# DeltaNet followed by a GELU MLP on one core: 32 heads in lockstep on 64x64 tiles, the MLP interleaved, the order list-scheduled

## The chip, the cores and the metric

The kernel runs on one core of one Trainium2 chip. The metric is the device time of one execution in microseconds; lower is better. A run more than 1.5% above the fastest of its kernel counts as slow; ratios use the other, fast runs alone, medians are of all runs. One core has five engines that matter here: TensorE (matmuls, PE in the profile, PEld for its weight loads), VectorE (DVE), ScalarE (ACT), GpSimd (POOL) and SyncE (SP, which here only issues DMA transfers).

## The reference

```python
# q, k, v: (4 batches, 8 heads, 768 tokens, 48); beta: (4, 8, 768)
k_n = k / (np.linalg.norm(k, axis=-1, keepdims=True) + 1e-06)
for t in range(S):                       # S = 768 tokens, one after the other
    y[:, :, t] = einsum('bhd,bhde->bhe', q[:, :, t], state)
    v_old = einsum('bhde,bhd->bhe', state, kt)
    state = state + bt * einsum('bhd,bhe->bhde', kt, vt - v_old)
# x: (3072 tokens, 384) from y, heads side by side
h = x @ w_in                             # 384 -> 2048
g = 0.5 * h * (1 + tanh(c * (h + 0.044715 * h**3)))
return g @ w_out                         # 2048 -> 384
```

Both kernels take 64 tokens at a time (a chunk). Inside a chunk the recurrence becomes a triangular 64x64 system, whose inverse is built by repeated squaring: M and N are the powers of the matrix and of its transpose, L is the inverse so far. Five levels of matmul and eviction (reading the product out of PSUM) follow one another. Only then come the few matmuls with the state S, which one chunk hands to the next: R = v - K S, U = T R, and S + KᵀU.

## The kernel before

Two heads are put on the diagonal of one 128x128 matrix (a pair), so half of every product and of every eviction, the two off-diagonal blocks, is zeros. A column is 8 pairs of one chunk; three columns are in flight. The five levels:

```python
for lev in range(1, 6):                              # cut
    for hf in range(NHALF):                          # two halves of 4 pairs
        for jj in range(NSLOT):
            E("pe", f_matmul(b0[:, jj, :], Nsrc[:, jj, :], Msrc[:, jj, :]), ...)   # 128x128x128
            if not last:
                E("pe", f_matmul(b1[:, jj, :], Msrc[:, jj, :], Nsrc[:, jj, :]), ...)
    yield
    ...
        E("act", f_act(Mdst[:, :, :], b0[:, :, :]), ...)     # evictions of 128x512
        ...
            E("pe", f_matmul(b1[:, jj, :], Mdst[:, jj, :], prev[:, jj, :]), ...)
        E("dve", f_tt(cur[:, :, :], b1[:, :, :], prev[:, :, :], ALU.add), ...)     # LT
    yield
```

The norm is a square and a sum, then a square root on ScalarE and an addition and a reciprocal on VectorE:

```python
E("pool", f_tt(sq_col[:, :, :], Kcv, Kcv, ALU.mult), ...)
E("dve", f_reduce(n1[:, :], sq_col[:, :, :], AX.X, ALU.add), ...)
E("act", f_act(n2[:, :], n1[:, :], ACT.Sqrt), ...)
E("dve", f_tscalar(n1[:, :], n2[:, :], 1e-6, ALU.add), ...)
E("dve", f_recip(n2[:, :], n1[:, :]), ...)
```

All columns are done before the MLP starts. Its GELU is a sigmoid form: two passes of ScalarE and three of VectorE for each block of 128x512.

```python
while nxt < len(tasks) or active:                    # DeltaNet: at most three columns
    while nxt < len(tasks) and len(active) < 3: ...
...                                                  # then the MLP, block by block
E("act", f_act(gb["hs"], hbk), ...)
E("dve", f_stt(gb["gq"], gb["hs"], two_ca, gb["hs"], ALU.mult, ALU.mult), ...)
E("dve", f_stt(gb["garg"], gb["gq"], two_c, gb["hs"], ALU.add, ALU.mult), ...)
E("act", f_act(gb["gs"], gb["garg"], ACT.Sigmoid), ...)
E("dve", f_tt(gb["gT"], gb["gs"], gb["hs"], ALU.mult), ...)
```

## Time and profile before

| | us |
|---|---|
| median of the first 3 runs | 963.94 (956.53 to 969.27) |
| loading, TensorE nearly idle | 0 to 74 |
| DeltaNet | 74 to 667 |
| MLP | 667 to 960 |

From the page of the kernel before: busy time of each engine, TensorE's busy tenths and its granted clock in 40 equal slices of the span, and the chain of work that ended last.

```profile
span 960.0 us, 14337 instructions
PE 569.2 (59%) x5459; PEld 415.1 (43%) x5472; DVE 532.3 (55%) x940; ACT 422.6 (44%) x866; POOL 218.7 (23%) x187
PE   0003667675667663767676768676566656556563
PEclk9999968786787687686776766587667879897987
...
PE 38%; DVE 24%; ACT 12%; issue 10%; SPq 6%; POOL 5%; DMA 3%; DVEq 0%; POOLq 0%; ACTq 0%
```

No engine is near full, and the chain of waits jumps between three of them. After the loading, the clock is rarely at nine or ten tenths. (Its records are only full or half; "warm" below means full clock.) The windows view of the kernel before gives busy us and instructions of each engine in the three stages, then the clock and the DMA share:

```profile
core 0: us, PE busy (x) PEld busy (x) DVE busy (x) ACT busy (x) POOL busy (x), PEclk, DMA share, GB/s
0.00:74.00 74.00, 3.88 (x32) 3.45 (x32) 10.39 (x7) 1.70 (x3) 21.53 (x22) 1.00 0.60 94
74.00:667.00 593.00, 392.58 (x4763) 342.76 (x4764) 360.29 (x642) 294.62 (x643) 197.12 (x165) 0.75 0.13 27
667.00:960.00 293.00, 172.76 (x668) 68.86 (x678) 161.65 (x291) 126.24 (x221) 0.00 (x0) 0.81 0.06 20
```

And three of its costliest groups (line, engine, operation, out<-in, shapes, count | busy us, mean ns | idle before it):

```profile
L134 ACT ACTIVATE MA<-mb 128x512 bf16<-128x512 f32 x240 | 134.6, 604 | 148.0 <-PE mb L118 147.0
L130 DVE SCALAR_TENSOR_TENSOR Kres<-Kres 128x512 bf16<-128x512 bf16 x192 | 127.3, 688 | 87.8 <-ACT Kres L134 86.5
L126 DVE TENSOR_TENSOR LT<-mb,LT 128x512 bf16<-128x512 f32 x192 | 123.4, 686 | 77.3 <-PE mb L118 77.3
```

Each of these 128x512 passes costs 0.60 us on ScalarE and 0.69 us on VectorE. The change attacks the number of these passes.

### The profile page before, as it was taken

The page shows a single profiled execution, that of the slowest core. Times are in us where ns is not written, and L with a number is a line of the kernel's source. Part 1 is how long each engine was busy: PE and PEld are TensorE (multiplying, and loading weights), DVE is VectorE, ACT ScalarE, POOL GpSimd, SP SyncE. Part 2 cuts the span into 40 slices and gives each one's busy share as a digit, 9 for nine tenths or more (in the row PEclk, how much of TensorE's full clock was granted, in tenths as well). Part 3 has the DMA queues.
Part 4 walks back from the last instruction along what each step waited for, and adds up shares of the span by engine and source line. Part 5 has one row for each costly group of instructions (what it writes and reads, how often), then busy time and mean ns, then how long its engine had stood idle before and what let it go on. Part 6 is the DMA issues. An engine that isn't in the chain of part 4 may idle for free.

```text
span 960.0 us, 14337 instructions
## 1 busy us (share of the span) xinstructions
PE 569.2 (59%) x5459; PEld 415.1 (43%) x5472; DVE 532.3 (55%) x940; ACT 422.6 (44%) x866; POOL 218.7 (23%) x187
## 2 busy tenths in 40 slices
PE   0003667675667663767676768676566656556563
PEld 0002656564556553656565656664222212222221
DVE  3102757574666574667575757565545547474654
ACT  0002545553546452554545454455434434453443
POOL 3405052523333214415151515030000000000000
PEclk9999968786787687686776766587667879897987
DMA  7554002154000001530000000000001000000000
GB/s 103 97 82 138 11 21 71 33 103 78 1 6 1 5 2 27 82 48 2 1 1 2 1 2 1 2 13 15 15 15 44 1 33 1 33 8 26 14 20 33
DMA packets 119990, 28.57 MB, mean 30 GB/s; under 512 B 114417, under 2 KB 119537, under 8 KB 119537
## 3 DMA queue, kind: packets, MB, share of 16 engines
q1 hardware_dynamic: 107120, 26.44, 13.0%
q10 hardware_dynamic: 12800, 1.21, 1.0%
q8 instruction: 43, 0.70, 0.3%
q14 instruction: 27, 0.21, 0.1%
HBM read 20.55 MB, written 4.72 MB: 26 GB/s over the span
## 4 chain that ended last, share of the span: by engine, by line
PE 38%; DVE 24%; ACT 12%; issue 10%; SPq 6%; POOL 5%; DMA 3%; DVEq 0%; POOLq 0%; ACTq 0%
PE mb L118 37%; SPq L163 6%; DVE LT L126 6%; ACT Kres L134 6%; DVE Kres L130 5%; DVE NB L138 3%; DMA out_dram<-Kres 3%; DVE Kres L126 2%; ACT QT L134 2%; PE mb L122 2%; POOL IMN L126 2%; ACT KnT L134 2%; POOL sq_col L126 2%; DVE MA L126 2%; DVE NB L126 1%
## 5 line engine op out<-in xcount | busy, mean ns | idle before, releaser
L134 ACT ACTIVATE MA<-mb 128x512 bf16<-128x512 f32 x240 | 134.6, 604 | 148.0 <-PE mb L118 147.0
L130 DVE SCALAR_TENSOR_TENSOR Kres<-Kres 128x512 bf16<-128x512 bf16 x192 | 127.3, 688 | 87.8 <-ACT Kres L134 86.5
L126 DVE TENSOR_TENSOR LT<-mb,LT 128x512 bf16<-128x512 f32 x192 | 123.4, 686 | 77.3 <-PE mb L118 77.3
L118 PE MATMUL mb<-W,Kres 128*128 128x384 bf16 x384 | 99.7, 397 | 108.8 <-DVE Kres L126 80.0
L118 PE MATMUL mb<-MA,NB 128*128 128x128 bf16 x960 | 145.5, 254 | 0.0
L118 PE MATMUL mb<-NB,MA 128*128 128x128 bf16 x768 | 125.9, 253 | 8.8 <-DVE LT L126 8.3
L134 ACT ACTIVATE Kres<-mb 128x512 bf16<-128x512 f32 (+1 forms) x120 | 68.2, 574 | 113.2 <-PE mb L118 83.1
L118 PEld LDWEIGHTS mb<-W,Kres 128*128 128x128 bf16 x384 | 36.6, 111 | 173.9 <-DVE Kres L126 127.3
L118 PE MATMUL mb<-LT,MA 128*128 128x128 bf16 x768 | 68.5, 238 | 64.1 <-DVE NB L138 61.5
L118 PEld LDWEIGHTS mb<-MA,NB 128*128 128x128 bf16 x960 | 104.4, 117 | 0.0
L118 PEld LDWEIGHTS mb<-NB,MA 128*128 128x128 bf16 x768 | 87.7, 116 | 20.6 <-DVE LT L126 13.8
L118 PEld LDWEIGHTS mb<-LT,MA 128*128 128x128 bf16 x768 | 52.0, 107 | 74.9 <-ACT NB L134 43.2
L134 ACT ACTIVATE Kres<-Kres 128x512 bf16<-128x512 bf16 x96 | 59.8, 628 | 50.9 <-DVE Kres L130 50.8
L122 PE MATMUL mb<-identb,Qb_col 128*96 128x128 bf16 x192 | 38.9, 292 | 56.9 <-POOL Qb_col L138 56.9
L122 PE MATMUL mb<-identb,Kb_col 128*96 128x128 bf16 x192 | 27.9, 293 | 72.6 <-ACT QT L134 72.6
L138 DVE CAST NB<-mb 128x512 bf16<-128x512 f32 x96 | 65.1, 678 | 3.6 <-PE mb L118 3.6
L126 POOL TENSOR_TENSOR IMN<-ident,NB 128x512 bf16<-128x512 f32 x48 | 55.2, 1156 | 30.7 <-DVE NB L126 30.0
L122 PEld LDWEIGHTS mb<-identb,Qb_col 128*96 128x96 bf16 x192 | 34.2, 181 | 57.5 <-POOL Qb_col L138 57.5
L134 ACT ACTIVATE NB<-mb 128x512 bf16<-128x512 f32 x96 | 58.6, 611 | 0.0
L126 DVE TENSOR_TENSOR Kres<-Kres 128x512 bf16<-128x512 bf16 x96 | 40.0, 422 | 32.3 <-ACT Kres L134 29.6
L122 PEld LDWEIGHTS mb<-identb,Kb_col 128*96 128x96 bf16 x192 | 19.1, 169 | 80.9 <-ACT QT L134 80.9
L118 PE MATMUL mb<-Vres,W 128*128 128x512 bf16 x184 | 53.0, 414 | 0.9 <-issue 0.7
(70 smaller groups left out, 1059.5 us busy)
## 6 DMA issues: line engine op xcount, KB each, us to landing
Qres<-in_q_dram SPq DMA_DIRECT2D x64, 72.0 KB, 2.5
Kres<-in_k_dram SPq DMA_DIRECT2D x64, 72.0 KB, 2.6
out_dram<-Kres SPq DMA_DIRECT2D x24, 192.0 KB, 1.9
Vres<-in_v_dram SPq DMA_DIRECT2D x48, 72.0 KB, 2.6
xsb<-in_moe_w_in_dram SPq DMA_DIRECT2D x3, 1024.0 KB, 4.9
xsb<-in_moe_w_out_dram SPq DMA_DIRECT2D x3, 960.0 KB, 5.2
Vres<-in_v_dram ACTq DMA_DIRECT2D x16, 72.0 KB, 2.9
Bres<-in_beta_dram SPq DMA_DIRECT2D x48, 1.5 KB, 2.4
```

What stands on the lines that cost most here:

```text
L118: return lambda t: t.matmul(out, lhsT, rhs, start=start, stop=stop)
L122: return lambda t: t.transpose(out, in_, idm)
L126: return lambda e: e.tensor_tensor(out, a, b, op)
L130: return lambda e: e.scalar_tensor_tensor(out, in0, scalar, in1, op0, op1)
L134: return lambda s: s.activation(out, in_, func)
L138: return lambda e: e.tensor_copy(out, in_)
L163: return lambda sp: sp.dma_start(out, in_)
```

## The change

The intent has five parts. Heads no longer share a 128x128 matrix: each head's 64x64 product runs on one quarter (tile) of the array, so a 128x512 eviction carries 16 heads' matrices and no zeros. All 32 heads of a chunk go together through 12 chunks. Loads are per chunk, so the work starts after the first chunk's loads. The MLP of finished tokens is interleaved, with one GELU pass on ScalarE. And the order of every engine is fixed in advance by a list scheduler from planned durations; each engine's queue then runs in that order, with waits where a result is needed.

The diff rewrites the whole file; this is its core, with cuts.

```diff
+LAT = {"pe": 0.25, "dve": 0.12, "act": 0.14, "pool": 0.16, "sp": 0.0}
+class Plan:                                          # list scheduler, cut
+    def op(self, cost, fns, reads=(), writes=(), prio=0.0, alloc=(), dma=None, lat=0.0):
+...
+def mm_pe(n_ins, cols):                              # planned duration of small matmuls
+    return {"pe": 0.02 + n_ins * max(0.030, (cols / 2.4 + 32) * 0.5e-3)}
+...
+# the norm: the square root has become a power on GpSimd
+op({"pool": 0.6}, {"pool": f_tt(sr[j], ss[j], half, ALU.pow)}, ...)
+op({"dve": 0.1}, {"dve": lambda e: e.tensor_scalar(ss[j], sr[j], 1e-6, None, op0=ALU.add)}, ...)
+op({"dve": 0.2}, {"dve": lambda e: e.reciprocal(rn[j], ss[j])}, ...)
+# K and Q of 32 heads are transposed by one DMA, issued by SyncE
+op({"sp": 1.1}, {"sp": f_dma(KQT[i]..., KQ[i]..., True)}, ..., lat=4.0)
+...
+def nl(...):                                         # one level: N and L of 8 pairs
+    return [(bank(h1, p // 4)[64*a:64*a+64, ...], M[64*a:64*a+64, p, :],
+             NL[64*a:64*a+64, p, :, :]..., True, True, True)
+            for p in range(8) for a in range(2)]     # a alternates: two tiles of the array
+...
+# GELU in one pass
+op({"act": 0.6}, {"act": f_act(G[:, fc, :], lambda h=h: bank(h), ACT.Gelu_apprx_tanh)}, ...)
-E("dve", f_stt(gb["gq"], gb["hs"], two_ca, gb["hs"], ALU.mult, ALU.mult), ...)
-E("dve", f_stt(gb["garg"], gb["gq"], two_c, gb["hs"], ALU.add, ALU.mult), ...)
-E("act", f_act(gb["gs"], gb["garg"], ACT.Sigmoid), ...)
```

## The prediction

> **What bounds the kernel now.** No engine: the page gives TensorE 59% busy, VectorE 55%, ScalarE 44%. Three phases follow one another (windows view): loading, 0–74 us, with TensorE almost idle; DeltaNet, 74–667 us (TensorE 393 us busy, VectorE 360, ScalarE 295); MLP, 667–960 us (TensorE 173, VectorE 162, ScalarE 126). The chain of waits is 38% TensorE, 24% VectorE, 12% ScalarE: one dependency chain of matmul, eviction, matmul, filled by only three columns in flight. The granted clock is 0.75 in DeltaNet and 0.81 in the MLP: start to start, a 128-column matmul takes 56 ns warm and 107 ns cold, a 48-column one 25 and 40 ns (my reading of start times). The Trainium skill, "TensorE: Matmul & The Clock Gate", Part 1, names these two states; the clock records here are only 1.0 and 0.5, so they agree.
>
> **What the change does.**
> - 64x64 tiles instead of block-diagonal 128x128 pairs: an eviction of 128x512 now carries 8 useful pairs, not 4. PSUM-reading VectorE work falls from 480 large passes to 274 (274 x 0.685 us = 188 us); 34+12 passes of 768 columns (about 0.95 us, estimated from 349 ns at 192 and 685 ns at 512) are 44 us; the rest about 28 us: **VectorE 260 us** (532 before).
> - Gelu becomes one ScalarE pass; two STT (688 ns), a multiply (422 ns) and a copy per tile go. **ScalarE about 150 us** (230 x 0.60 plus small; 423 before).
> - GpSimd: 24 x 1.16, 24 x 1.47, 12 x 0.82, 24 masks of 1024 at about 2 us: **about 125 us**.
> - TensorE: 5,474 matmuls become 7,107. 4,896 of 48 or 64 columns at 27–30 ns, 1,536 of 128 columns at 40–45 ns (estimates from the warm 25 and 56 ns, two tiles overlapping), MLP 288 x 0.216 + 384 x 0.163 = 125 us: **about 340 us warm**, more when cold. TensorE becomes the fullest engine, about 28 us per chunk of 64 tokens with its MLP share.
> - MLP runs inside DeltaNet, so its 293 us stop being a separate phase; only the last tile (16 gelu blocks, 4 output blocks) remains as a tail.
> - Loading shrinks to the first chunk: first matmuls near 28 us instead of 74.
>
> **Sum.** Start 28 us (load, norm, GpSimd scaling, one DMA transpose of 16 blocks, estimated 4–8 us), then 320 us of TensorE work, tail 35 us (DMA transpose, 21 us matmuls, output): 383 us if TensorE never waited warm. It will wait: fixed order from planned costs, eight PSUM banks, six matmul–eviction levels, a clock I expect at 0.75–0.9, and switches between 64x64 and 128x128, which drain the array (the Trainium skill, "TensorEngine Tiling (Array Packing)", Key Properties; no run here shows it yet). I take TensorE progress at about 80%: 320/0.8 = 400, so **465 us, 405 to 545**. Chances: faster 0.985, same 0.01, slower 0.005.
>
> **What would show it.** TensorE busiest, above 65%; VectorE 50–60% of the span; ScalarE about a third; small matmuls 27–30 ns apart warm; gelu blocks spread from about 90 us on; first matmul near 28 us; a tail of about 35 us without small matmuls.
>
> **What would make it wrong.** Small matmuls without the fast weight load costing 50 ns or more (span near 560); a 16-block DMA transpose taking 16 us of the SyncE queue and starving the chunks; a slow power operation or masks on GpSimd; a clock stuck at half; or a nearly always warm array (near 400).

## The result, and the profile after

The changed kernel takes 403.64 us (median of 4 runs, 401.96 to 405.79), the kernel before 963.51 us in the same rounds. The ratio is 0.4198, 95% interval 0.4170 to 0.4226. A ratio is the mean time of one kernel's fast runs over that of the other's of the same rounds, so it is not quite the ratio of the medians quoted. Where two changed kernels from different rounds are compared below, I give medians, and ratios where they tell something else. The time lies below the predicted 465 us and just outside the range of 405 to 545.

The same parts of the page, of the changed kernel:

```profile
span 404.1 us, 15305 instructions
PE 293.8 (73%) x7110; PEld 195.6 (48%) x7110; DVE 256.3 (63%) x389; ACT 146.7 (36%) x247; POOL 163.5 (40%) x112
PE   0100062646668969869978979989889999889997
PEclk9999997568588888998979999999999999999999
...
PE 40%; DVE 23%; POOL 20%; DMA 6%; SPq 4%; issue 4%; ACT 1%; DVEq 0%; POOLq 0%
```

TensorE is the fullest engine and, from about a third of the span on, nearly always at work with a warm clock. GpSimd has become a fifth of the chain. The windows view of the changed kernel, cut at the first small matmul, the first MLP matmul and the last small matmul:

```profile
0.00:52.00 52.00, 1.67 (x10) 1.37 (x10) 7.88 (x18) 1.28 (x1) 25.86 (x26) 1.00 0.96 169
52.00:123.00 71.00, 42.86 (x1458) 38.52 (x1460) 57.50 (x83) 25.09 (x44) 51.59 (x32) 0.72 0.77 138
123.00:371.00 248.00, 219.20 (x5480) 139.39 (x5480) 185.52 (x280) 109.94 (x186) 86.00 (x55) 0.96 0.38 71
371.00:404.00 33.00, 30.07 (x176) 16.36 (x168) 5.42 (x9) 10.36 (x17) 0.00 (x0) 1.00 0.19 61
```

Three stages thus answer the three terms of the prediction: a start of 52 us with the DMA engines at 96%, a middle of 319 us (52 to 371), and a tail of 33 us. Groups of the changed kernel that answer those of before:

```profile
L278 ACT ACTIVATE M<-ps 128x512 bf16<-128x512 f32 x90 | 52.8, 596 | 76.5 <-PE ps L285 76.1
L278 ACT ACTIVATE gT<-ps 128x512 bf16<-128x512 f32 x96 | 57.3, 597 | 62.5 <-PE ps L285 60.2
L269 DVE TENSOR_TENSOR NL<-ps,NL 128x512 bf16<-128x512 f32 x96 | 64.4, 684 | 2.9 <-PE ps L285 1.3
L269 POOL TENSOR_TENSOR sr<-ss,half 128x16 f32<-128x16 f32 x12 | 34.9, 2906 | 10.3 <-DVE ss L469 10.3
```

A pass costs what it cost before; there are fewer. The last line is the power on GpSimd, 2.9 us for 16 columns, which the plan had at 0.6.

**How small matmuls are spaced.** Busy time is no measure of this, because matmuls overlap in the record. I read start to start, within blocks of equal matmuls at full clock:

| | columns | tiles alternated | ns per matmul | count |
|---|---|---|---|---|
| M and N levels, L | 64 | 2 | 16.4 | 3,072 |
| N with L side by side | 128 | 2 | 28 | 1,152 |
| K Kᵀ and Q Kᵀ | 128 | 4 | 13.5 | 384 |
| with the state, K S, Q S, KᵀU | 48 | 4 | 8.2 to 8.4 | 1,056 |
| T R, D U | 48 | 2 | about 16 | 768 |
| MLP | 512, 384 | 1 | 216, 163 | 288, 384 |

Two matmuls on different tiles often start 3 to 6 ns apart; the next pair follows about 30 to 50 ns later. The Trainium skill, "TensorE: Matmul & The Clock Gate", Part 3 ("The mechanism", and the span model after it), says that matmuls at different tile positions overlap and start about 4 ns apart; the trace agrees. Summed, all small matmuls are 108.7 us of warm work; with the 95 us of the MLP's work that lie in the middle it is 203.6 us. A switch between the two kinds costs time too: from a small to an MLP matmul it takes 125 ns where the spacing would be about 29, and back 309 where it would be 216, so about 0.095 us each and 16 us for 170 of them. The skill, "TensorEngine Tiling (Array Packing)", "Key Properties", says that changing the tiling mode drains the array; a cost at each switch agrees with that.

So the middle of 319 us is 203.6 us of work, 16 of switches, 62.9 in gaps over 0.4 us, and 36 in the rest (half clock and small gaps). This split is worked out from the start times, with the spacings of the table.

### The profile page after: what moved, and what is told of

Its sections match the earlier page's. It is cut to its first block, busy times and chain, and to the rows that moved or that the text cites. A ratio compares the mean times of both kernels' runs of the same rounds, so it can differ in the third digit from the quotient of the medians.

```text
span 404.1 us, 15305 instructions
## 1 busy us (share of the span) xinstructions
PE 293.8 (73%) x7110; PEld 195.6 (48%) x7110; DVE 256.3 (63%) x389; ACT 146.7 (36%) x247; POOL 163.5 (40%) x112
## 4 chain that ended last, share of the span: by engine, by line
PE 40%; DVE 23%; POOL 20%; DMA 6%; SPq 4%; issue 4%; ACT 1%; DVEq 0%; POOLq 0%
PE ps L285 40%; POOL sr L269 8%; DVE NL L269 6%; POOL ML L269 5%; SPq L293 4%; DMA KQT<-KQ 3%; DVE NL L274 3%; POOL NU L269 3%; DVE M L269 2%; DMA kf<-in_k_dram 2%; POOL sq L269 2%; DVE ss L473 2%; DVE S L269 2%; POOL NL L269 1%; DVE ss L469 1%
## 5 line engine op out<-in xcount | busy, mean ns | idle before, releaser
L285 PE MATMUL ps<-NL,M 64*64 64x128 bf16 (+1 forms) x2304 | 81.5, 219 | 32.0 <-DVE NL L269 22.6
L285 PEld LDWEIGHTS ps<-NL,M 64*64 64x64 bf16 x2304 | 64.9, 118 | 53.3 <-DVE NL L269 31.2
L278 ACT ACTIVATE M<-ps 128x512 bf16<-128x512 f32 x90 | 52.8, 596 | 76.5 <-PE ps L285 76.1
L278 ACT ACTIVATE gT<-ps 128x512 bf16<-128x512 f32 x96 | 57.3, 597 | 62.5 <-PE ps L285 60.2
L285 PE MATMUL ps<-xT,W 128*128 128x512 bf16 x288 | 76.6, 401 | 2.4 <-DVE S L269 1.2
L285 PE MATMUL ps<-W,gT 128*128 128x384 bf16 x384 | 69.8, 331 | 1.7 <-DVE TT L269 0.8
L269 DVE TENSOR_TENSOR NL<-ps,NL 128x512 bf16<-128x512 f32 x96 | 64.4, 684 | 2.9 <-PE ps L285 1.3
L285 PE MATMUL ps<-M,NL 64*64 64x64 bf16 x1920 | 54.9, 202 | 10.2 <-issue 2.9
L278 ACT ACTIVATE NL<-ps 128x512 bf16<-128x512 f32 x44 | 26.2, 597 | 85.7 <-PE ps L285 85.4
L285 PEld LDWEIGHTS ps<-M,NL 64*64 64x64 bf16 x1920 | 44.6, 117 | 22.6 <-issue 7.3
L285 PEld LDWEIGHTS ps<-W,gT 128*128 128x128 bf16 x384 | 35.2, 99 | 25.4 <-issue 1.0
L269 POOL TENSOR_TENSOR sr<-ss,half 128x16 f32<-128x16 f32 x12 | 34.9, 2906 | 10.3 <-DVE ss L469 10.3
L269 DVE TENSOR_TENSOR M<-ps,ML 128x512 bf16<-128x512 f32 x24 | 16.3, 682 | 15.9 <-PE ps L285 15.9
```

The source lines that it names most:

```text
L269: return lambda e: e.tensor_tensor(out() if callable(out) else out, a() if callable(a) else a, b() if callable(b) else b, op)
L278: return lambda e: e.activation(out, a() if callable(a) else a, func)
L285: ins = t.matmul(out, lhsT, rhs, start=st, stop=sp_, skip_group_check=skip)
```

## Experiments

All kernels gave the correct result but one, which says so. Their order of running is that of their numbers.

| kernel | median us | ratio to before (95% interval) |
|---|---|---|
| changed kernel | 403.64 | 0.4198 (0.4170 to 0.4226) |
| e1 tiles one after another | 427.03 | 0.4433 (0.4410 to 0.4456) |
| e2 weights late | 403.84 | 0.4199 (0.4178 to 0.4220) |
| e3 transpose first | 403.57 | 0.4190 (0.4166 to 0.4214) |
| e4 power of -0.5 | 395.55 | 0.4107 (0.4088 to 0.4126) |
| e5 small matmuls doubled | 520.22 | 0.5413 (0.5385 to 0.5442) |
| e6 planned with measured durations | 379.00 | 0.3949 (0.3927 to 0.3971) |
| e7 outputs on ScalarE | 399.43 | 0.4156 (0.4135 to 0.4176) |
| e8 power, weights, transposes | 407.17 | 0.4221 (0.4188 to 0.4254) |
| e9 only TensorE's durations corrected | 381.02 | 0.3944 (0.3929 to 0.3958) |
| e10 all others corrected | 380.71 | 0.3940 (0.3929 to 0.3950) |
| e11 e6 with power of -0.5 | 373.98 | 0.3881 (0.3860 to 0.3901) |
| e12 less MLP work (wrong result) | 388.56 | 0.4024 (0.4001 to 0.4047) |
| e13 norm four places later | 393.67 | 0.4117 (0.4087 to 0.4147) |
| e14 another order, wrong durations | 404.42 | 0.4236 (0.4214 to 0.4259) |
| e15 e11 with an early start | 366.37 | 0.3837 (0.3813 to 0.3860) |
| e16 e15, one row sum later | 368.54 | 0.3830 (0.3807 to 0.3852) |
| e17 e14 with the norm later | 394.37 | 0.4072 (0.4049 to 0.4095) |
| e18 e16, one transpose earlier | 363.65 | 0.3764 (0.3745 to 0.3783) |

### The price of TensorE's work: e1, e12, e5

**e1** keeps the plan and every instruction, but orders the matmuls inside a block so that one tile's come after the other's.

```diff
-                                for p in range(8) for a in range(2)]
+                                for a in range(2) for p in range(8)]
```

> The small matmuls of every operation are sorted so that those on the same 64x64 tile follow one another; the order of operations on every engine is unchanged and the result must be the same. Theory A (the prediction missed because neighbouring matmuls on different tiles run at the same time, and TensorE is what the middle waits for): a 64-column matmul goes from 16 ns to 27-30 ns of start-to-start, a 128-column one from 28 to 53-56, about 105 us more TensorE work, and the time rises by 60 to 105 us, into the predicted range (463 to 508 us). Theory B (matmul cost does not matter, the evictions and GpSimd set the pace and the forecast only allowed too much waiting): the matmuls slow down as said but the time rises by less than 25 us.

Measured: over a block, 64 columns now take 25 ns and 128 columns 42 ns, and the small matmuls sum to 174 us, 66 us more. A block of each kernel (start, from first start to last end, count; the last matmul alone is about 0.19 of it), first the changed kernel, then e1:

```profile
172.84 0.44 PE L285 MATMUL ps<-NL,M 64*64 64x64 bf16 x16
178.30 0.59 PE L285 MATMUL ps<-NL,M 64*64 64x64 bf16 x16
```

These are means. Inside such a block of e1 the starts lie 53, 31, 32, 32, 6, 25, 27, 5, 27, 5, 26, 32, 32, 31, 32 ns apart, and the starts of neighbouring operations mix in the same way. I read this as two streams, one for each tile (the trace does not name the tile): each runs at 31 to 32 ns, and the second begins before the first has ended. With 128 columns the same reading gives 55 to 56 ns. So one tile alone costs about 32 ns for 48 or 64 columns and 56 for 128, and e1 takes away only a part of the overlap. The time rose by 23 us only. So the alternation of tiles is what makes the small matmuls cheap, and theory A, that this price sets the time nearly one for one, fell. The added work filled gaps: those over 0.4 us in the middle went from 62.9 to 30.3 us.

**e12** goes the other way: 192 of the 288 first-layer matmuls are left out (the result is wrong), which is 192 x 0.216 = 41 us less work for TensorE.

```diff
-                                     ... kt == 0, kt == KT - 1, False) for kt in range(KT)]
+                                     ... kt == 0, kt == 0, False) for kt in range(1)]
```

> Wrong result on purpose: of the three 512-column matmuls of each first-layer block only one is issued, 192 matmuls or 41 us of warm TensorE work less, no instruction or wait added and every other order kept. It asks what a microsecond of TensorE work is worth without the doubt of e5_double, whose 11,000 more instructions left 64 us of gaps that no semaphore explains. Theory A (work over 0.8): -50 us. Theory B (as in e1_serial, about a third shows in the middle, all of it in the tail): -15 to -25 us.

Measured: 15 us less, 3 of them in the tail. Per microsecond of TensorE work the time moved by 23/66 = 0.35 in e1 and 15/41 = 0.37 here. About a third, in both directions: work and waits are not proportional, and most of a change in work is absorbed by waits of TensorE for other engines.

**e5** issues the small matmuls of six of the eight kinds twice (not Q S and D U).

```diff
+            if twice and skip and st and sp_:
+                t.matmul(out, lhsT, rhs, start=st, stop=sp_, skip_group_check=skip)
```

> Each small matmul of six of the eight kinds is issued twice with the same operands (the second overwrites), which adds about 100 us of warm TensorE work at the measured 8 to 28 ns apiece: the small matmuls then cost about 207 us, what the prediction had assumed (213). Order and result unchanged. Theory A (the time is TensorE work over 0.8, as the prediction summed): +125 us, about 529. Theory B (waiting is not in proportion to work: as in e1_serial, where 66 us more work cost 23 us, most of it falls into waits): +35 to +65 us, 440 to 468.

Measured: 117 us more, for about 100 us of added work. That would be a slope over 1, but the experiment is spoilt: the kernel has 26,697 instructions, and TensorE stands for 64 us in gaps that no semaphore explains (3.5 us in the changed kernel), some in the middle of a block of equal matmuls. I suspected the supply of instructions, and no run tests it. The trace supports it: of the 44 such gaps over 0.4 us, 43 end 1.2 to 1.6 us after the end of a packet of the instruction queue, and moments taken at random lie so in 8% of cases (worked out from the DMA packets). So this run gives no slope, and the slope of about a third (e1, e12) is shown only for up to 66 us of added work.

### VectorE standing at the norm: e4, e13, e14, e17

The changed kernel, around 176 us. The columns are start, duration, engine, line, operation; the idle time before it and what ended it are in brackets:

```profile
174.88 0.95 DVE L469 TENSOR_REDUCE ss<-sq 128x16 f32<-128x768 f32 x1 [1.92 <-POOL sq L269]
175.75 0.68 DVE L269 TENSOR_TENSOR TT<-ps,NL 128x512 bf16<-128x512 f32 x1
175.91 2.90 POOL L269 TENSOR_TENSOR sr<-ss,half 128x16 f32<-128x16 f32 x1 [1.07 <-DVE ss L469]
178.85 0.18 DVE L473 TENSOR_SCALAR ss<-sr 128x16 f32<-128x16 f32 x1 [2.42 <-POOL sr L269]
178.93 0.68 DVE L274 CAST NL<-ps 128x512 bf16<-128x512 f32 x1
179.65 0.69 DVE L269 TENSOR_TENSOR NL<-ps,NL 128x512 bf16<-128x512 f32 x1
180.40 0.63 PE L285 MATMUL ps<-NL,M 64*64 64x128 bf16 x16 [2.43 <-DVE NL L269]
```

VectorE has the addition of the norm (L473) next in its queue and stands for 2.4 us until GpSimd's power is done. The evictions of NL behind it had nothing to wait for, and TensorE loses the same 2.4 us. The Trainium skill, "PSUM — Partial Sum Buffer", "Engine vs sequencer instructions", says that VectorE's queue is strictly first in, first out; the trace agrees.

**e4** takes the power of -0.5 instead of 0.5, so that the addition of 1e-6 and the reciprocal go (the result stays correct); the order of all else stays.

```diff
-        op({"dve": 0.1}, {"dve": lambda e: e.memset(half[:, :], 0.5)}, ...)
+        op({"dve": 0.1}, {"dve": lambda e: e.memset(half[:, :], -0.5)}, ...)
+            P.orders["dve"].remove(t_.idx)     # the addition
+            P.orders["dve"].remove(r_.idx)     # the reciprocal
```

> GpSimd takes the power -0.5 directly; the add and the reciprocal on VectorE go (24 operations, 15 us of VectorE busy time, about 1.4 us per chunk of the chain norm to transpose); the order of everything else is kept. Theory P (the chain of preparation through GpSimd limits the chunks up to 250 us, where the chain of waits shows 20% GpSimd): the time falls by 6 to 15 us. Rival (preparation has slack, TensorE sets the pace): less than 3 us.

Measured: 8 us less. TensorE's wait for NL fell from 22.6 us over the whole run to 9.8 us (us in total, times, longest us; the changed kernel, then e4):

```profile
PE ps L285 <- DVE NL L269: 22.6, 29, 3.8
PE ps L285 <- DVE NL L269: 9.8, 22, 1.6
```

But e4 also shortens the chain that prepares a chunk, so it doesn't say which of the two helped.

**e13** keeps both operations and the plan, and moves them four places down VectorE's queue, from the third chunk on. That makes the preparation longer, not shorter.

```diff
+        for c_, t_, r_ in NORM:
+            if c_ < 2: continue
+            at = o_.index(t_); o_.remove(t_); o_.insert(at + 4, t_)
+            ...                                 # the reciprocal right behind it or where it was
```

> The order of the changed kernel, but from the third chunk on the addition and reciprocal of each norm stand four places later in VectorE's queue. Theory H (VectorE stands at the norm's addition waiting for GpSimd's power, and the evictions behind it keep TensorE waiting): the wait of the addition for the power falls from 10.3 us to under 4, TensorE's wait for the normalised rows does not rise by as much, and the time is 390 to 399. Theory P (the length of the preparation chain limits the chunks, not what stands behind it): the norm comes later still, TensorE waits longer for it, and the time is 403 or more.

Measured: 10 us less (8 by the ratios). Theory P fell, H held. The waits of VectorE in the changed kernel (engine, line waited for: us in total, times, longest us):

```profile
DVE ss L473 <- POOL sr L269: 19.9, 11, 3.8
```

and in e13, where the one of 3.8 us belongs to the second chunk, which was not moved:

```profile
DVE ss L473 <- POOL sr L269: 4.2, 2, 3.8
```

**e14** asks whether the first order was merely unlucky: another order from the same wrong durations.

```diff
-        STEP = 28.0
+        STEP = 24.0
```

> Another order, planned with the same wrong durations as the changed kernel; only the planner's constant for how chunks' priorities are staggered goes from 28 to 24. Theory unlucky draw (any new order avoids the bad places): 378 to 388, as the other re-planned kernels. Theory corrections matter (an order from wrong durations is as bad as another): 397 to 410.

Measured: no faster, and its wait at the norm is the same:

```profile
DVE ss L473 <- POOL sr L269: 18.9, 11, 3.8
```

**e17** moves the norm in this order too, with the edit of e13.

> The step kernel (404.42 us) with the same edit as the norm-later kernel: additions and reciprocals of the norms four places later in VectorE's queue from the third chunk on. If VectorE standing at the addition is a cost of any order planned with a too cheap power: 6 to 10 us less, 394 to 399, with the wait for the power down from 18.9 us to under 6. If the gain of the norm-later kernel was a matter of its one order: 401 or more.

Measured: 10 us less (394.37 against 404.42; the ratios, from different rounds, give 16). The same wait in e17:

```profile
DVE ss L473 <- POOL sr L269: 4.7, 2, 3.8
```

So in two orders the same small move wins about 10 us. A plan that has the power at 0.6 us puts the addition too early in an in-order queue. The move changes one thing more. Six of the twelve additions of the changed kernel last 0.8 to 3.7 us instead of 0.17; each starts just after an operation of GpSimd and ends within 0.04 us of the end of one (the longest runs from 64.91 to 68.64 us, beside two of GpSimd from 64.85 to 68.61). Together the twelve take 12.1 us, in e13 6.7. So the gain is that of the addition's place; how much of it is the wait and how much the longer addition was not separated. The profiled run of e17 was one of the slow state, by 1.5%; I take no more from it than this wait.

### What the plan's durations are worth: e6, e9, e10, e11, e7

**e6** gives the scheduler the durations of the trace, and plans anew.

```diff
-            return {"pe": 0.02 + n_ins * max(0.030, (cols / 2.4 + 32) * 0.5e-3)}
+            return {"pe": 0.02 + n_ins * {128: 0.028, 64: 0.0164, 48: 0.012}[cols]}
-            op({"pool": 0.6}, {"pool": f_tt(sr[j][:, :], ss[j][:, :], half[:, :], ALU.pow)},
+            op({"pool": 2.9}, {"pool": f_tt(sr[j][:, :], ss[j][:, :], half[:, :], ALU.pow)},
-                    op({"sp": 0.6}, {"sp": f_dma(t[s]..., lat=4.0)
+                    op({"sp": 1.0}, {"sp": f_dma(t[s]..., lat=5.0)
```

(also the addition 0.6, the DMA transposes 3.1 and 1.8 on SyncE, a ScalarE pass of 512 columns 0.60, MLP matmuls 0.84 and 1.49.)

> The same operations, planned again with durations as the trace shows them (small matmuls 16/28/12 ns instead of 30/43/30, power on GpSimd 2.9 us instead of 0.6, DMA issue 1.0 and transpose 3.1 us on SyncE, ScalarE eviction 0.60). Theory W (the waits of the middle come from an order planned with wrong costs): the time falls by 10 us or more, to 393 or less. Rival (the order is good enough; waits come from chains and buffers): within 5 us of 404.

Measured: 379.00 us, nearly 25 less, with the same operations. (The planner may choose ScalarE or VectorE for some evictions: VectorE has 374 operations here, 379 in e9 and 390 in e10, against 389.) The chain of e6 is that of a kernel which waits for its main engine:

```profile
PE 65%; DVE 12%; SPq 7%; POOL 5%; issue 5%; DMA 4%; ACT 2%
```

**e9** corrects only the TensorE durations, **e10** only the others.

> Planned again with only the TensorE durations corrected (16, 28 and 12 ns per small matmul, and about 0.19 us more per MLP operation for the change of tile mode). e6_replan, with all durations corrected, took 379 us against 404. Theory X (plan and prediction share one error, the price of a small matmul): most of the 25 us come from it, 376 to 390 us. Rival Y (the wrong GpSimd and DMA durations mattered): 395 us or more.

> Planned again with every duration corrected but those of TensorE. Theory X: 395 us or more. Rival Y: 376 to 390 us.

Measured: 381.02 and 380.71. Each alone gives nearly the whole gain, so both theories fell as I had stated them. What the three good orders share is that VectorE no longer stands long at the norm (over the whole run 3.8 us in e6, 10.3 in e9, 4.8 in e10, against 19.9), and that TensorE's waits for NL between 110 and 360 us fell from 14.8 us to at most 6. e13 shows that the norm's place alone is worth about 10 of the 24 us. Which re-ordering brings the other 14 was not isolated. A shift of evictions off VectorE is not needed for it, as e10 has none, and e14, one other order from the wrong durations, does not bring it.

**e11** is e6 with the power of -0.5, planned without the addition and the reciprocal.

> e6_replan with the power -0.5 taken directly, planned without the add and the reciprocal on VectorE. If the two gains are of different causes (order; length of the preparation chain) they add up: 371 us or less. If both only relieve the same wait of the middle: 375 to 380 us. Meant also as the best version so far.

Measured: 373.98 us, 5 us less than e6, between the two expectations.

**e7** lets the outputs and x leave PSUM on ScalarE alone, which is less busy than VectorE (36% against 63%).

```diff
-   op(d_any(DM), {"act": f_act(osb[o_]...), "dve": f_cp(osb[o_]...)}, ...)
+   op({"act": 0.49}, {"act": f_act(osb[o_]...)}, ...)
```

> All evictions of MLP outputs and of x go to ScalarE (33 operations, about 23 us of VectorE busy time, move from VectorE at 63% to ScalarE at 36%); planned with the old costs. Theory D (VectorE is a second limiter): the time falls by 5 to 12 us. Rival (VectorE has slack): less than 3 us, either way.

Measured: 4 us less, between the two. The plan was made anew, so this is no clean price of VectorE's time.

### The late start: e2, e3, e8, e15, e16, e18

The first small matmul came at 52 us, not at the 28 I predicted. In the changed kernel K and Q of the first chunk are ready to be transposed at 33.8 us, but the transpose stands behind the loads of later chunks in SyncE's queue and is issued at 47.0:

```profile
45.66 1.32 SPq L293 DMA_DIRECT2D vf<-in_v_dram  x1
47.02 3.12 SPq L292 DMA_TRANSPOSE KQT<-KQ  x1
```

**e2** issues the weight loads after the scaling of the second chunk; **e3** puts the first transpose ahead of those loads.

```diff
+        at = o_.index(KQQ[1]) + 1                                       # e2, GpSimd's queue
+        o_[at:at] = wt
+        at = max(n for n, i in enumerate(o_) if P.ops[i].dma == "d_br1") + 1   # e3, SyncE's
+        o_[at:at] = t0
```

> The five weight loads are issued by GpSimd after the scaling of the second chunk instead of in the first microseconds; nothing else is moved. Theory S (the late start, first small matmul at 52 us against 28 predicted, comes from DMA engines that are full: the weights share them with the first chunks): the first small matmul comes at 40-45 us and the time falls by 6 to 12 us. Theory G (the start is set by the chain of GpSimd operations): first small matmul within 3 us of 52 and the time within 3 us.

> The DMA transpose of the first chunk is moved ahead of the loads of the third and fourth chunk in the SyncE queue. Its input is ready at 33.8 us and it is issued at 47.0. Theory Q (it stood behind load issues in an in-order queue): it is issued at about 34 us, first small matmul at 40-42 us, the time falls by 5 to 11 us. Theory S alone (only bytes in flight matter): the landing takes longer and the first matmul moves by less than 4 us.

Measured: the first small matmul came 12 and 13 us earlier (40.5 and 39.1 us), and the time did not change at all. The first U came at 80.2 and 78.5 us, against 80.3. TensorE's fixed order has matmuls of the second chunk between those of the first, and the second chunk's transpose came as late as before: its issue ended at 70.6 and 70.5 us, against 72.3, and TensorE stood for it for 17 us instead of 9.

**e8** joins the power of -0.5, late weights, and transposes ahead of later loads.

> e4_rpow with the weights late and the DMA transposes of chunks 0 to 9 ahead of the loads of later chunks in the SyncE queue. e2 and e3 alone brought the first small matmul to 40 us but gained nothing. Theory C (the matmul order of chunk 0 holds operations of chunk 1, whose transpose was still late; both must come early): the first U eviction moves from about 80 to 60-70 us and the time from 395.5 to 378-390 us. Rival (what follows sets the pace and takes any gain back): within 3 us of 395.5.

Measured: the first small matmul at 26.8 us, the first U at 67.2, and in the end 407 us (its four fast runs average 404.9), no faster than the changed kernel and 9 to 12 slower than e4, so both theories fell. The second chunk's transpose took 15.9 us to issue on SyncE, next to the weights, and the gain was gone by the third U (135.6 us, against 129.5 in the changed kernel). A start that serves one chunk only moves the wait.

**e15** therefore serves the first two chunks: on top of e11, transposes first in SyncE's priorities, loads of a later chunk after the scaling of the chunk before, weights after the scaling of the third.

```diff
-                load_step(c + 2, T(c - 1))
+                load_step(c + 2, T(c - 1), [f"KQq{(c + 1) % RB}"])
-               writes=[f"KQT{i}"], prio=pr + 0.2, ...
+               writes=[f"KQT{i}"], prio=pr - 60, ...
+                    op({"pool": 1.2}, {"pool": f_dma(W1[:, kt, :], ...)}, reads=["KQq2"], ...
```

> The re-planned kernel with the power of -0.5 (373.98 us), and the loads ordered so that chunks 0 and 1 are both served early: transposes ahead of later loads, loads of later chunks after the scaling of the chunk before, weights after that of chunk 2. Theory start (the late start was lost time): first product U at 60 to 65 us instead of about 78, and 355 to 368 us. Rival (the start is limited by what must be moved, and an earlier chunk 0 only waits for chunk 1): within 3 us of 374, or slower.

Measured: the first U at 43.0 us and the second at 62.9, 32 and 37 us earlier than in e11, and yet only 4 (ratios) to 8 us (medians) in the end. The loss is in the third chunk: its U came at 103.7 us, 41 us after the second and only 18 us ahead of e11's; at the last U the lead is 10 us. In that stretch VectorE stood 9.4 us at the row sum of the fourth chunk's squares, whose loads shared the DMA engines with the weights:

```profile
DVE ss L463 <- POOL sq L269: 9.4, 1, 9.4
```

**e16** moves that row sum six places down.

```diff
+        at = o_.index(SUM[3]); o_.remove(SUM[3])
+        o_.insert(at + 6, SUM[3])
```

> The start kernel (366.37 us), with the row sum of the fourth chunk's squares six places later in VectorE's queue, so that the evictions of the third chunk stand ahead of it. Theory blocked queue: VectorE's 9.4 us wait for the squares is gone, the third chunk's U, at 103.7 us in the start kernel, comes 6 to 10 us earlier, and the time is 358 to 363. Rival (the bytes of the loads and weights limit the first 100 us, and the fourth chunk only comes later): within 2 us of 366, or slower.

Measured: VectorE's wait is gone, and nothing is won; the theory fell. The next in-order queue had taken over. SyncE's queue in e16 (start, time to issue, x count of transfers):

```profile
59.54 1.86 SPq L292 DMA_TRANSPOSE KQT<-KQ  x1
61.44 3.64 SPq L293 DMA_DIRECT2D kf<-in_k_dram  x2
65.12 13.89 SPq L293 DMA_DIRECT2D qf<-in_q_dram  x2
79.06 5.55 SPq L293 DMA_DIRECT2D vf<-in_v_dram  x2
84.66 1.88 SPq L293 DMA_DIRECT2D brow<-in_beta_dram  x2
86.66 3.85 SPq L292 DMA_TRANSPOSE xT<-x  x1
```

and TensorE's at the same time:

```profile
79.72 0.95 PE L285 MATMUL ps<-NL,M 64*64 64x128 bf16 x14
93.11 1.44 PE L285 MATMUL ps<-xT,W 128*128 128x512 bf16 x3 [12.44 <-issue]
94.48 0.63 PE L285 MATMUL ps<-M,NL 64*64 64x64 bf16 x16
```

TensorE's next matmuls are the first of the MLP; they need the transpose of x. The rows of x were written by 66.4 us, but the transpose was issued at 86.66, behind the loads of q, v and beta of the fourth chunk. The chunk's own matmuls stand behind. (The view calls this wait "issue"; that it is the transpose is my reading from its issue at 86.66 plus a landing time of 6.4 us, which gives 93.1.)

**e18** moves that transpose alone.

```diff
+        xt = [i for i in o_ if P.ops[i].dma == "d_x0"]
+        o_.remove(xt[0])
+        at = min(n for n, i in enumerate(o_) if P.ops[i].dma == "d_qf3")
+        o_.insert(at, xt[0])
```

> The sum-later kernel (368.54 us, ratio 0.383) with the first transpose of the MLP's input moved ahead of the loads of q, v and beta of the fourth chunk in SyncE's queue. Theory blocked queue (TensorE's order has the first matmuls of the MLP ahead of the third chunk's, and they wait for this transpose): the first matmul of the MLP comes at 73 to 80 us instead of 93, the third chunk's U 8 to 15 us earlier than 104, and the time is 355 to 363. Rival (the bytes limit; the fourth chunk comes as much later as the third comes earlier): within 2 us of 366 to 368.

SyncE's queue in e18:

```profile
62.95 2.03 SPq L293 DMA_DIRECT2D kf<-in_k_dram  x2
66.50 14.38 SPq L292 DMA_TRANSPOSE xT<-x  x1
80.93 3.38 SPq L293 DMA_DIRECT2D qf<-in_q_dram  x2
```

Measured: the first MLP matmul at 85.7 us instead of 93.1, the third U at 97.1 instead of 104.2, and 363.65 us, 5 us less than e16. The place in SyncE's queue held TensorE, as the theory said; the sizes fell short, by a little in the time and more in the first matmul, because the transpose now took 14.4 us to issue while the weights were moving. In this stretch of e18 (63 to 104 us) the DMA engines are busy 96% of the time and TensorE 27.6 of 41 us:

```profile
63.00:104.00 41.00, 27.60 (x697) 19.65 (x691) 21.80 (x31) 16.22 (x26) 13.68 (x9) 0.67 0.96 156
```

This is the best version: its ratio to the kernel before is 0.3764, about 10% less time than the changed kernel (0.3764 / 0.4198 = 0.897).

## Why the prediction was right or wrong

The direction, the engines and the tail were right; the time was 61 us too high and just outside the range. Term by term, as the prediction put its sum:

| term | predicted us | measured us |
|---|---|---|
| start | 28 | 52 |
| TensorE work of the middle, warm | 320 | 203.6 |
| share of the middle in which TensorE progresses | 0.80 | 203.6 / 319 = 0.64 |
| middle | 400 | 319 |
| tail | 35 | 33 |
| sum | 463 | 404 |

**The step that failed** is the price of the small matmuls: "4,896 of 48 or 64 columns at 27–30 ns, 1,536 of 128 columns at 40–45 ns", with "two tiles overlapping". By these ranges that is 194 to 216 us, and I reckon it as 213. They took 108.7. The overlap of tiles was named, but far too small: for 128 columns I had gone from the 56 ns of the kernel before to 40 to 45, and for 48 and 64 columns from its 25 ns up. e1 shows what the overlap is worth. One tile alone takes about 32 and 56 ns, which would be some 243 us for all small matmuls (an estimate from e1's start times). With the tiles one after another, which still overlap in part, they are 174 us, and that kernel, at 427 us, is inside my range. With tiles alternating, they cost 16.4 and 28 ns on two tiles and 8 to 14 on four. So my price held some 30 us of overlap where there were about 134, and that is the 104 us by which it was too high. The MLP's part was right: 125 us in the whole run, 216 and 163 ns.

**What compounded it** is the division by 0.8, "320/0.8 = 400". Put into that formula, the right work would have given 203.6 / 0.8 = 254.5 us for the middle, 64 us less than measured, so the waits were under-estimated at the same time as the work was over-estimated. With the right work the whole sum would have been 28 + 254.5 + 35, about 318 us, and further off, on the other side: that 465 came as near as it did is two errors that partly cancel, which is luck. A fixed share is the wrong form. e1 and e12 show that a microsecond of TensorE work is worth 0.35 to 0.37 us of time here, as most of it falls into waits: in e1 the middle is 339 us for about 270 us of work, a share of 0.80; in the changed kernel 0.64. At that slope my excess of 116 us of work (320 against 203.6) is worth about 41 of the 61 us by which the time was too high (an estimate, beyond the 66 us that e1 added).

**The start was mis-sized the other way**, 52 us against 28, by the queue of loads on SyncE in front of the first transpose. It did not make the prediction wrong: taking 12 us from it alone (e2, e3) changed nothing.

**What the prediction named and the trace confirmed:** VectorE 260 us (256.3), ScalarE 150 (146.7), a tail of 35 (33), TensorE the fullest engine (73%), transposes of 4 to 8 us (5 to 7 to landing), and a cost at each switch between tile modes (0.095 us), which I had named as a drain. GpSimd was 163.5 instead of 125 us: the power, 34.9 us, was not in my count, though I had named "a slow power operation or masks on GpSimd" as a risk. The MLP started at 123.5 us rather than at about 90.

**What would have held it in the range:** with "a nearly always warm array (near 400)" I had named the case that happened from 123 us on (clock 0.96, where I had expected 0.75 to 0.9; before, from 52 us, it was 0.72), but gave it no room below 405.

**What the waits of the changed kernel are:** shown by e13, e14 and e17 is that about 10 us of them come from the place of the norm's addition in VectorE's queue, planned for a power of 0.6 us where the real one takes 2.9; there VectorE stands for the power, and some additions themselves are long. Shown by e6 is that 25 us go when the plan uses measured durations; e9 and e10 show that either half of the corrections suffices, and I can't say what brings the 14 us beyond the norm. Shown by e15, e16 and e18 is that the start can be had only in part (10 us of the 32 by which the first U came earlier), and that one in-order queue after another holds the next chunk. How much of the rest is the DMA engines themselves, 96% busy from 63 to 104 us in e15 and e18, was not separated.

## What to carry to other kernels

Read the price of a matmul from the start times of a stream like the one you will build, with the same tiles alternating, and don't turn work into time with one share: change the work by a known amount in both directions and read the slope. In a kernel with a fixed order, a duration that the planner has too low is paid by what stands behind it in an in-order queue, not by the operation itself, so put measured durations into the plan and look for an engine that waits while the next entry of its queue is ready. An earlier start is worth something only when the second and third chunk come earlier as well; follow one result, here U, from chunk to chunk to see where it is given back.

## What the Trainium skill lacked or had wrong

- "TensorE: Matmul & The Clock Gate", Part 1, says that start to start never drops below about 25 ns however small the matmul is. That does not hold for tiles in turn: 16.4 ns over two, 8.2 to 8.4 ns over four, each matmul with its own weights. (On one tile the starts of e1 are 31 to 32 ns apart for 48 and 64 columns.) Part 3 of the page says that tiles overlap, but Part 1 does not point to it, and no sustained spacing for such streams of small matmuls is given.
- "TensorEngine Tiling (Array Packing)", "Key Properties", names the drain at a change of tiling mode without a figure: about 0.095 us each here, 170 times.
- "GPSIMD Engine Reference" has no figure for a power: 2.9 us for 128x16, more than twice a subtraction of 128x512 (1.16 us).
- On no page did I find how much longer a DMA transpose holds the issuing queue beside other transfers: 1.3 to 5.2 us in the changed kernel, 11.8 us (e2), 14.4 us (e18) and 15.9 us (e8) beside the weight loads.
